# Constant loads placed behind the first input of a Fourier mixer with an MLP

## The chip, the cores and the metric

The kernel runs on one core of a Trainium2 chip. A core has TensorE (PE, matmuls into PSUM), VectorE (DVE) and ScalarE (ACT), which move results from PSUM to SBUF and do elementwise work, GpSimd (POOL) and SyncE (SP). POOL and SP issue most DMAs; 16 DMA engines carry all of them. The metric is the time of one execution on the device in microseconds (us). Before the change it is 810.49 us, the median of three runs from 810.40 to 810.59.

## The reference

Two layers in a row, on 8 sequences of 3008 positions with 256 channels, all float32:

```python
X = np.fft.rfft(x, axis=1)
Yr = Xr @ w_r - Xi @ w_i + b_r
Yi = Xr @ w_i + Xi @ w_r + b_i
Y  = soft_threshold(Yr, 0.01) + 1j * soft_threshold(Yi, 0.01)
y  = np.fft.irfft(Y, n=3008, axis=1)
...
h = y.reshape(24064, 256) @ w_in          # 256 -> 2048
out = (s * relu(h) ** 2 + b) @ w_out      # 2048 -> 256
```

## The kernel before, in words

**The transform as matmuls.** 3008 is 94 x 32, and each transform goes in two steps. The first is a matrix of 94 rows and 96 columns, `A_t` (23 pairs of frequencies and two real ones, as 24 pairs), applied to x viewed as 94 rows of 32 x 256 values. The second, of length 32 with the twiddle factors in it, has a matrix of its own for each of the 24 pairs q: `F_t` for the real and `F_2` for the imaginary part of the input, and `T_t` for the way back. `C_t` is the last step of the inverse. Everything goes through TensorE in float16 with float32 sums.

**Batch 0 goes alone.** The other batches are spread in small units between the MLP's matmuls of the batch before; their order is written out by hand, and a planner's table says which engine takes which piece of work. Batch 0 has nothing to hide behind, and `first_batch` treats it differently: it mixes the channels between the two forward steps. Its stages are

1. first step: for each group of four n2 (a group is half a tile `x16`, which holds eight), four matmuls for each half of the channels put 384 columns into one bank, and the bank is copied to `ut` by ScalarE or VectorE (`evac`, lines 237 and 239, which picks the engine with less planned work). After each group follow five filler matmuls on a tile of ones (`keep_awake`);
2. for each half of the output channels and each of six groups of four pairs: `mix` (eight matmuls of `ut` with the mixing weights `W_t`; the results leave as `g` on VectorE, with the bias `b_g`, line 620, and on ScalarE, line 617), `fwd_dft` (two matmuls for each pair with `F_t` and `F_2`, and one matmul with the selector `sel_t`, a part of the tile `small`, that adds the bias row `b_h`), the soft threshold (ScalarE line 647, VectorE line 649), and `inv_dft` with `T_t`;
3. the turn with an identity (`eye_t`) and the last step with `C_t`, with the first units of batch 1 between them. The first matmul of the MLP, with `w_in`, follows.

**The loads of batch 0.** POOL issues x in eight pieces of four n2 each (line 367), because these loads turn float32 into float16; then two bias rows (line 406). SP issues, in this order, `A_t` (line 385), the mixing weights `w_r` and `w_i` into `w_st` (line 391), four bias rows (line 399), the first part of `F_c` (line 422) and `sel_t` (line 428). `F_c` is the compact form of the forward matrices of pairs 0 to 11: `place_w` (line 480) turns the weights into float16 on ScalarE, and `place_f` (lines 487 to 491) puts the blocks of `F_c` into `F_t` and `F_2`, which were cleared before. A copy of one half goes through ScalarE, the other through VectorE, and the part for `F_2` is four operations on VectorE.

**What holds loads back.** The kernel delays a load by a tiny write: a memset of one element of the destination is queued on VectorE behind a certain eviction, and the DMA must wait for that memset. After the second tile of x, the second part of `F_c` (pairs 4 to 11) is let go in this way (line 586), and the weights are placed; after the third tile the tables `T_t`, `F_t` for pairs 12 to 23, `F_2[1]` and the rest (lines 431 to 441, memsets at line 580), and the first part of `F_c` is placed. The second part of `F_c` is placed after the evictions of the first `mix`. POOL waits with x of batch 1 and the weights of the MLP for the arrival of that `F_t` (a copy of one element, line 591).

**What sets the order.** Up to the end of `first_batch` the framework orders each engine's instructions: in the order of the text, unless an instruction isn't ready by the framework's own estimate and a later one is. `tc.issue_after` adds an order by hand. Behind `first_batch` the order is the written one.

Of the kernel before, what the change touches and what calls it, by code (L numbers as in the profile page):

```python
# [15 lines left out]
P = 128  # L16
N1 = 94
N2 = 32
# [131 lines left out]
def kernel(  # L150
# [13 lines left out]
    nc = tc.nc  # L164
    B, S, D = x.shape
# [5 lines left out]
    H = NPAIR // 2  # L171
# [4 lines left out]
    A_d = nc.inline_tensor(first.astype(np.float16), name="dft_first").ap()  # L176
# [46 lines left out]
    def matmul(out, lhs, rhs, **how):  # L223
        pump()
        return nc.tensor.matmul(out, lhs, rhs, **how)  # L225
# [7 lines left out]
    def evac(dst, src, cols):  # L233
        ta, td = over["act"] + cols / 1200.0, over["dve"] + cols / 960.0
        if act_first(ta, td):
            work("act", ta)
            return None, nc.scalar.copy(out=dst, in_=src)
        work("dve", td)
        return nc.vector.tensor_copy(out=dst, in_=src), None
# [66 lines left out]
    def mix_bank():  # L306
        return track("psm", 4, pools["m"].tile([P, 512], F32, name="psm", tag="psm"))
# [13 lines left out]
    def one_bank():  # L321
        return track("psf", 2, fpool.tile([P, 512], F32, name="psf", tag="psf"))
# [8 lines left out]
    XCH = 8  # L331
# [25 lines left out]
    def emit_load_x(b, chunks=range(N2 // XCH)):  # L357
        xv = x[b].rearrange("(n1 n2) d -> n1 (n2 d)", n2=N2)
        for c in chunks:
            if b < 2 and c == N2 // XCH - 1:  # L360
                t = x2pool.tile([P, XCH * D], F16, name="x2", tag="x2")
            else:
                t = xpool.tile([P, XCH * D], F16, name="x16", tag="x16")
            parts = 2 if b == 0 else 1
            w = XCH * D // parts
            for i in range(parts):
                nc.gpsimd.dma_start(
                    out=t[0:N1, i * w : (i + 1) * w],
                    in_=xv[:, c * XCH * D + i * w : c * XCH * D + (i + 1) * w],
                )  # L370
            x16[(b, c)] = t

# [3 lines left out]
    def keep_awake(n):  # L376

        ps = other_bank()
        for _ in range(n):
            mm = matmul(ps[:, 0:P], ones, ones, start=True, stop=True)  # L380
        return mm


    A_t = cpool.tile([P, 96], F16, name="A_t")
    nc.sync.dma_start(out=A_t[0:N1, :], in_=A_d)
    emit_load_x(0)
    W_t = cpool.tile([P, DC, 2, D], F16, name="W_t")
    w_st = []
    for w in (w_r, w_i):
        st = rpool.tile([P, DC, D], F32, name="w_st", tag="rt")  # L390
        nc.sync.dma_start(out=st, in_=w.rearrange("(c p) e -> p c e", p=P))
        w_st.append(st)

    b_g = tpool.tile([P, 2, D], F32, name="b_g", tag="tail")
# [5 lines left out]
    F_c = uspool.tile([P, H, 2, N2], F16, name="F_c", tag="us")  # L400
    F_2 = [uspool.tile([P, H, P], F16, name="F_2", tag="us") for _ in range(2)]
# [5 lines left out]
    sel_t = small[:, 1, 0:P]  # L407
# [10 lines left out]
    F_t = cpool.tile([P, NPAIR, P], F16, name="F_t")  # L418
    T_t = cpool.tile([P, NPAIR, P], F16, name="T_t")

    def load_f_c(q):
        nc.sync.dma_start(out=F_c[:, q].rearrange("p q r k -> p q (r k)"), in_=F_d[:, q])

    load_f_c(slice(0, 4))

    def emit_load_forward():
        load_f_c(slice(4, H))
        nc.sync.dma_start(out=sel_t, in_=S_d)

    def emit_load_inverse():  # L430
        nc.sync.dma_start(out=T_t[:, 0:H], in_=t_d[:, 0:H])
        nc.sync.dma_start(out=F_t[:, H:], in_=f_d)
        nc.sync.dma_start(out=F_2[1], in_=f_2_d)
        t_load = nc.sync.dma_start(out=T_t[:, H:], in_=t_d[:, H:])
        with tc.issue_after(t_load.ins):
            nc.sync.dma_start(out=eye_t, in_=E_d)
            nc.sync.dma_start(out=C_t, in_=C_d)
            for i, bv in enumerate((b_r, b_i)):
                nc.sync.dma_start(out=b_st[:, i], in_=bv.unsqueeze(0).to_broadcast([P, D]))
            nc.sync.dma_start(out=s_bc, in_=moe_s.unsqueeze(0).to_broadcast([P, 1]))  # L440
            nc.sync.dma_start(out=bb_bc, in_=moe_b.unsqueeze(0).to_broadcast([P, 1]))
# [36 lines left out]
    def place_w():  # L478
        for i in range(2):
            nc.scalar.copy(out=W_t[:, :, i], in_=w_st[i])  # L480

    def place_f(q):

        for a in range(2):
            r = slice(64 * a, 64 * a + 64)
            copy = nc.scalar.copy if a else nc.vector.tensor_copy
            copy(out=blocks(F_t)[r, q, :, a], in_=F_c[r, q])
            nc.vector.tensor_scalar_mul(
                out=blocks(F_2[0])[r, q, 0, a], in0=F_c[r, q, 1], scalar1=-1.0
            )  # L490
            nc.vector.tensor_copy(out=blocks(F_2[0])[r, q, 1, a], in_=F_c[r, q, 0])
# [58 lines left out]
    def first_batch():  # L550
        ut = ypool.tile([P, DC, 96, N2], F16, name="ut", tag="yt")
        last_dve = last_act = None
        last_pe = keep_awake(40)
        for g in range(N2 // 4):
            c, h = divmod(g, 2)
            for dc in range(DC):
                ps = one_bank() if dc else mix_bank()
                with tc.issue_after(last_pe.ins):
                    for j in range(4):
                        lo = (4 * h + j) * D + dc * P  # L560
                        mm = matmul(
                            ps[:, j * 96 : j * 96 + 96],
                            x16[(0, c)][0:N1, lo : lo + P], A_t[0:N1, :],
                            start=True, stop=True,
                        )
                last_pe = mm
                on_dve, on_act = evac(
                    ut[:, dc, :, 4 * g : 4 * g + 4],
                    ps[:, 0:384].rearrange("p (n k) -> p k n", k=96), 384,
                )  # L570
                last_dve = on_dve or last_dve
                last_act = on_act or last_act
            with tc.issue_after(last_pe.ins):
                last_pe = keep_awake(5)
            if h == 0:
                continue
            if c == 2:
                with tc.issue_after(last_dve.ins):
                    for t in (T_t[:, 0:H], F_t[:, H:], F_2[1], T_t[:, H:]):
                        nc.vector.memset(t[0:1, 0, 0:1], 0.0)  # L580
                emit_load_inverse()
                with tc.issue_after(last_dve.ins), tc.issue_after(last_act.ins):
                    place_f(slice(0, 4))
            if c == 1:
                with tc.issue_after(last_dve.ins):
                    nc.vector.memset(F_c[0:1, 4, 0, 0:1], 0.0)
                emit_load_forward()
                with tc.issue_after(last_act.ins):
                    place_w()

        gate = nc.gpsimd.tensor_copy(out=w_in_t[0][0:1, 0:1], in_=F_t[0:1, H, 0:1])
        with tc.issue_after(gate.ins):
            emit_load_x(1)
            emit_load_weights()
# [128 lines left out]
        for i in range(2 * U + 2):  # L723
# [9 lines left out]
            k = i - U - 2  # L733
# [750 lines left out]
    with tc.tile_pool(name="psm", bufs=4, space=bass.MemoryType.PSUM) as pool:  # L1484
        pools["m"] = pool
        rest, more = first_batch()
# [27 lines left out]
    for b in range(2, B):  # L1514
        s0, s1, s2 = mark[b - 2], mark[b - 1], mark[b]
        p = s1 - s0
# [4 lines left out]
        p = s2 - s1  # L1521
# [11 lines left out]
    for ti in range(ti_n + 1):  # L1533
# [3 lines left out]
        for mc in range(MC):  # L1537
# [10 lines left out]
            n = max(len(units), 1)  # L1548
# [37 lines left out]
```

## Time and profile before

| | us |
|---|---|
| median of three runs | 810.49 |
| the profiled execution | 810.04 |
| its span, from the first to the last instruction | 808.2 |
| TensorE busy in the span | 799.2 |
| VectorE busy | 758.9 |
| ScalarE busy | 749.4 |
| first matmul on x | 5.39 |
| first mixing matmul | 14.54 |
| first matmul of the MLP | 44.85 |

How to read the profile: a timeline line gives the start, the duration, the engine, the line of the kernel, the operation, output <- inputs with their shapes, and how many instructions were merged into it; in brackets stands how long the engine was idle before it and what released it. PEld is TensorE's weight load, which lies beside the matmuls. SPq and POOLq are the issuing of DMAs. The lines of the DMA view give, for a stretch of time, each queue's packets, the MB that it moved, and the time of its packets as a share of all 16 DMA engines; q0 is POOL's queue, q1 is SP's. Matmuls and evictions go through helpers, so many have one line (225 for all matmuls) and are told apart by their tiles.

### The profile page before, as it was taken

Reading aid. Unit: us, or ns where it says so; the run is one execution under the profiler, and the core shown is the slowest. Engines: PE = TensorE matmul, PEld = TensorE weight load, DVE = VectorE, ACT = ScalarE, POOL = GpSimd, SP = SyncE. Lnnn points to the kernel's source line nnn. Section 1 sums busy time; section 2 is a strip of 40 time slices with the busy share of each in tenths; the row PEclk is TensorE's granted clock in tenths of the full one; section 3 lists DMA queues with packets and bytes.
Section 4 is the critical chain, followed back from the end, with each engine's and each line's share of the span. In section 5 each row is a group of like instructions: output and inputs, shape, how many; then the busy total and the mean of one; then the engine's idle time right before and its main releaser. Section 6 shows DMA issues by size and latency. Waiting matters only on the chain.

```text
span 808.2 us, 22126 instructions
## 1 busy us (share of the span) xinstructions
PE 799.2 (99%) x9006; PEld 613.1 (76%) x9006; DVE 758.9 (94%) x1342; ACT 749.4 (93%) x932; POOL 107.0 (13%) x151
## 2 busy tenths in 40 slices
PE   8999999999999999999999999999999999999998
PEld 7857767777777977788777886778867788777876
DVE  5899999999999999999999999999999999999895
ACT  5989999999999999999999999999999999998984
POOL 4540001110110101111011210012000100000000
PEclk9999999999999999999999999999999999999999
DMA  8983387555774658665686666666556434732213
GB/s 205 190 194 78 95 237 184 102 136 153 208 151 86 153 139 226 145 124 113 169 200 145 135 145 161 152 154 136 137 164 177 108 80 119 183 67 58 62 41 79
DMA packets 120766, 112.89 MB, mean 140 GB/s; under 512 B 9933, under 2 KB 98129, under 8 KB 120665
## 3 DMA queue, kind: packets, MB, share of 16 engines
q1 hardware_dynamic: 102409, 80.55, 36.0%
q0 software_dynamic: 18256, 30.94, 23.2%
q8 instruction: 70, 1.15, 0.6%
q14 instruction: 31, 0.25, 0.1%
HBM read 53.52 MB, written 46.66 MB: 124 GB/s over the span
## 4 chain that ended last, share of the span: by engine, by line
PE 93%; DMA 0%; ACT 0%; DVE 0%; issue 0%; DVEq 0%; ACTq 0%
PE psh L225 40%; PE psa L225 34%; PE psf L225 19%; DMA out_dram<-ost 0%; DVE ost L1278 0%; ACT rt L1154 0%; ACT u L288 0%; DVEq L1278 0%; ACTq L1154 0%
## 5 line engine op out<-in xcount | busy, mean ns | idle before, releaser
L225 PE MATMUL psh<-yt,w_in 128*128 128x512 f16 (+3 forms) x1792 | 444.5, 343 | 0.2 <-ACT rt L1154 0.2
L225 PEld LDWEIGHTS <-gt 128*128 128x128 f16 x4400 | 306.7, 98 | 141.7 <-DVE gt L1325 2.4
L1154 ACT ACTIVATE rt<-psh 128x1024 f32<-128x1024 f32 x339 | 346.9, 1025 | 23.7 <-PE psh L225 21.5
L1163 ACT ACTIVATE gt<-rt 128x1024 f16<-128x1024 f32 x277 | 289.6, 1059 | 3.1 <-DVE rt L1156 0.7
L225 PE MATMUL psa<-w_out_t,gt 128*128 128x128 f16 (+1 forms) x2208 | 199.6, 224 | 0.0
L225 PEld LDWEIGHTS <-w_in 128*128 128x128 f16 x1824 | 152.0, 98 | 15.8 <-issue 1.4
L225 PE MATMUL psa<-T_s,gt 128*128 128x128 f16 x1824 | 144.3, 219 | 0.0
L1317 POOL DMA_DIRECT2D gt<-gt x63 | 54.8, 870 | 650.0 <-DVE s L1325 194.3
L1165 DVE TENSOR_TENSOR gt<-rt 128x1024 f16<-128x1024 f32 x99 | 120.0, 1216 | 2.4 <-ACT rt L1154 2.1
L1390 DVE SCALAR_TENSOR_TENSOR ost<-psa,s_bc,bias_bc 128x256 f32<-128x256 f32 x152 | 72.6, 478 | 6.7 <-PE psa L225 5.7
L1325 DVE TENSOR_TENSOR gt<-gt 128x1024 f16<-128x1024 f16 x109 | 74.4, 682 | 0.7
L1390 DVE SCALAR_TENSOR_TENSOR ost<-psa,s_bc,ost 128x256 f32<-128x256 f32 x129 | 61.6, 477 | 4.0 <-PE psa L225 3.8
L1325 DVE TENSOR_TENSOR gt<-gt,s 128x1024 f16<-128x1024 f16 x86 | 58.8, 684 | 1.4 <-PE psf L225 0.8
L1325 DVE TENSOR_TENSOR s<-gt 128x1024 f16<-128x1024 f16 x86 | 58.7, 683 | 0.5 <-ACT gt L1163 0.2
L880 DVE TENSOR_TENSOR ring<-psf,s 128x512 f16<-128x512 f32 x84 | 57.5, 685 | 1.7 <-PE psf L225 1.0
L225 PEld LDWEIGHTS <-s 128*128 128x128 f16 x688 | 45.4, 98 | 17.6
L225 PE MATMUL psa<-T_s,s 128*128 128x128 f16 x688 | 52.4, 219 | 0.0
L225 PE MATMUL psf<-W_g,xf 128*128 128x256 f16 x336 | 50.4, 273 | 0.0
L1156 DVE TENSOR_SCALAR rt<-psh 128x1024 f32<-128x1024 f32 x37 | 45.0, 1219 | 3.3 <-PE psh L225 1.6
L225 PEld LDWEIGHTS <-xf 128*128 128x128 f16 x504 | 44.7, 98 | 3.3
L225 PE MATMUL psf<-x,A_t 94*96 94x512 f16 x103 | 39.3, 382 | 0.3 <-DVE u L288 0.2
L225 PE MATMUL psf<-C_t,vs 96*128 96x96 f16 x484 | 38.3, 205 | 0.3 <-DVE u L288 0.3
(116 smaller groups left out, 836.6 us busy)
## 6 DMA issues: line engine op xcount, KB each, us to landing
out_dram<-ost SPq DMA_DIRECT2D x74, 256.0 KB
gt<-gt POOLq DMA_DIRECT2D x63, 256.0 KB, 4.0
ud<-u SPq DMA_DIRECT2D x56, 192.0 KB
us<-ud SPq DMA_DIRECT2D x28, 384.0 KB
vd<-v SPq DMA_DIRECT2D x42, 256.0 KB
vs<-vd SPq DMA_DIRECT2D x28, 384.0 KB
x<-in_x_dram POOLq DMA_DIRECT2D x56, 188.0 KB, 5.6
ring<-ring SPq DMA_DIRECT2D x120, 64.0 KB
```

The lines of the kernel that those rows point to most:

```text
L225: return nc.tensor.matmul(out, lhs, rhs, **how)
L880: lambda e: nc.vector.tensor_tensor(out=ring[0][:, i % 4], in0=ps, in1=hold[i // 2][:, i % 2].unsqueeze(1).to_broadcast([P, 2, D]), op=ALU ...
L1154: nc.scalar.activation(out=rt, in_=ps, func=AF.Relu)
L1156: nc.vector.tensor_scalar(out=rt, in0=ps, scalar1=0.0, scalar2=None, op0=ALU.max)
L1163: nc.scalar.activation(out=gt, in_=rr, func=AF.Square)
L1165: nc.vector.tensor_tensor(out=gt, in0=rr, in1=rr, op=ALU.mult)
L1317: nc.gpsimd.dma_start(out=a12, in_=a11, accum_op=ALU.add)
L1325: nc.vector.tensor_tensor(out=out, in0=a, in1=b, op=op)
L1390: ins = nc.vector.scalar_tensor_tensor(out=out(), in0=hold[of], scalar=s_bc[0:size], in1=other(), op0=ALU.mult, op1=ALU.add,)
```

## The change

1. `A_t` is issued by SP between `w_r` and `w_i` instead of first.
2. The first part of `F_c` (pairs 0 to 3) is no longer issued at the start; it goes where the second part was, behind the memset after the second tile of x. The second part and `sel_t` go behind the third tile, ahead of the large tables, with memsets of their own.
3. The last piece of x (four n2) is loaded in two pieces of two, and the last group of the first step becomes two groups of two n2, each with its own evictions (192 columns) and its five fillers. The other loads of x keep their sizes.

```diff
-            parts = 2 if b == 0 else 1
-            w = XCH * D // parts
-            for i in range(parts):
+            ends = [0, XCH] if b else [0, 4, 6, 8] if c == N2 // XCH - 1 else [0, 4, 8]
+            for lo, hi in zip(ends, ends[1:]):
+                at = c * XCH * D
                 nc.gpsimd.dma_start(
-                    out=t[0:N1, i * w : (i + 1) * w],
-                    in_=xv[:, c * XCH * D + i * w : c * XCH * D + (i + 1) * w],
+                    out=t[0:N1, lo * D : hi * D], in_=xv[:, at + lo * D : at + hi * D]
                 )
...
     A_t = cpool.tile([P, 96], F16, name="A_t")
-    nc.sync.dma_start(out=A_t[0:N1, :], in_=A_d)
     emit_load_x(0)
...
         nc.sync.dma_start(out=st, in_=w.rearrange("(c p) e -> p c e", p=P))
+        if not w_st:
+            nc.sync.dma_start(out=A_t[0:N1, :], in_=A_d)
         w_st.append(st)
...
-    load_f_c(slice(0, 4))
-
     def emit_load_forward():
+        load_f_c(slice(0, 4))
+
+    def emit_load_inverse():
         load_f_c(slice(4, H))
         nc.sync.dma_start(out=sel_t, in_=S_d)
-
-    def emit_load_inverse():
         nc.sync.dma_start(out=T_t[:, 0:H], in_=t_d[:, 0:H])
...
-        for g in range(N2 // 4):
-            c, h = divmod(g, 2)
+        groups = [(lo, 4) for lo in range(0, N2 - 4, 4)] + [(N2 - 4, 2), (N2 - 2, 2)]
+        for n, k in groups:
+            c, at = divmod(n, XCH)
...
                 on_dve, on_act = evac(
-                    ut[:, dc, :, 4 * g : 4 * g + 4],
-                    ps[:, 0:384].rearrange("p (n k) -> p k n", k=96), 384,
+                    ut[:, dc, :, n : n + k],
+                    ps[:, 0 : 96 * k].rearrange("p (n k) -> p k n", k=96), 96 * k,
                 )
...
-            if h == 0:
+            if at == 0:
                 continue
             if c == 2:
                 with tc.issue_after(last_dve.ins):
-                    for t in (T_t[:, 0:H], F_t[:, H:], F_2[1], T_t[:, H:]):
-                        nc.vector.memset(t[0:1, 0, 0:1], 0.0)
+                    for t in (F_c[:, 4], sel_t, T_t[:, 0:H], F_t[:, H:], F_2[1], T_t[:, H:]):
+                        nc.vector.memset(t[0:1, 0:1, 0:1] if len(t.shape) > 2 else t[0:1, 0:1], 0.0)
                 emit_load_inverse()
...
             if c == 1:
                 with tc.issue_after(last_dve.ins):
-                    nc.vector.memset(F_c[0:1, 4, 0, 0:1], 0.0)
+                    nc.vector.memset(F_c[0:1, 0, 0, 0:1], 0.0)
                 emit_load_forward()
```

More of the change, by code (lines that the diff above doesn't have):

```diff
@@ L558, in first_batch @@
                 with tc.issue_after(last_pe.ins):
-                    for j in range(4):
-                        lo = (4 * h + j) * D + dc * P
+                    for j in range(k):
+                        lo = (at + j) * D + dc * P
                         mm = matmul(
```

## The prediction, made before the change was run

> **What bounds the kernel now.** I read the page's engine table first, then the end of the chain of waits, then the timeline of the first 20 us, where every line of the change lies, and last the DMA traffic of that stretch in short windows.
>
> ```profile
> span 808.2 us, 22126 instructions
> PE 799.2 (99%) x9006; PEld 613.1 (76%) x9006; DVE 758.9 (94%) x1342; ACT 749.4 (93%) x932; POOL 107.0 (13%) x151
> ...
> PE 93%; DMA 0%; ACT 0%; DVE 0%; issue 0%; DVEq 0%; ACTq 0%
> ...
> 44.59 0.04 issue
> ```
>
> TensorE is busy for 99% of the span, and the chain that ends last starts only at 44.59 us. The busy times by stretch say the same: from 44.6 to 800.0 TensorE is busy for 755.09 of 755.40 us. The change touches none of that; it can only move the moment at which that run begins. From 14.5 to 34.0 TensorE is busy for 19.27 of 19.50 us, and from 34.0 to 44.6 VectorE for 10.60 of 10.60. So what moves the first mixing matmul (14.54 us) moves the end by as much. Before it, the core waits for x of batch 0:
>
> ```profile
> 9.68 0.34 PE L225 MATMUL psm<-A_t,x 94*128 94x96 f16 x4 [0.28 <-DMA x<-in_x_dram]
> ...
> 13.62 0.34 PE L225 MATMUL psm<-A_t,x 94*128 94x96 f16 x4 [0.17 <-DMA x<-in_x_dram]
> ...
> 14.00 0.48 ACT L237 CAST ut<-psm 128x384 f16<-128x384 f32 x1 [0.49 <-PE psm L225]
> 14.54 1.92 PE L225 MATMUL psm<-W_t,ut 128*128 128x256 f16 x16
> ```
>
> The fourth piece of x is used at 9.68, the eighth at 13.62, each after a wait for its DMA. The last two evictions end at 14.48 (ScalarE) and 14.73 (VectorE), and the mix starts on the first. In the DMA windows 7.00 to 10.25 and 12.00 to 13.25 the columns are packets, MB, share of 16 engines:
>
> ```profile
> q0 software_dynamic: 336, 0.57, 94.9%
> q1 hardware_dynamic: 287, 0.10, 17.7%
> ```
>
> ```profile
> q0 software_dynamic: 122, 0.10, 48.6%
> q1 hardware_dynamic: 125, 0.11, 26.1%
> ```
>
> Queue q0 is x; q1 is SyncE's. The 0.10 MB of the first window are the first forward block (64 KB) and the selector (32 KB), issued at 3.45 and 3.85, and they move while x fills the engines. The 0.11 MB of the second are the second forward block (128 KB), issued at 10.84, at the tail of x.
>
> **The change part by part.**
>
> *Forward block 0 to 3 and selector out of x's way.* They took 17.7% of 3.25 us, 0.57 us of all 16 engines, 0.42 us of it before 9.25. What runs at x's tail instead, the 64 KB block, has 128 packets like the 128 KB one; the same 64 KB took about 0.3 us of all engines in the first window and the larger took 0.33 (26.1% of 1.25), so nothing is won or lost there. The fourth piece lands 0.42 us earlier, the eighth 0.57. That goes by engine share. If bytes bound x instead, the 96 KB go at the pace of its pieces (each read as 376 KB of float32 and landed as 188 KB of float16, 0.98 us apart: 13.62 less 9.68 over four) and give 0.25 us.
> The Trainium skill ("DMA: Bandwidth & Descriptors", section Specifications) puts the limit of HBM per core at about 358 GB/s, which would make bytes the bound and the saving 98,304 B / 358 GB/s = 0.27 us, so that the sum below would be 0.3 us higher. The rows here show 4 x 385 KB in 3.94 us, 391 GB/s, above that figure, so the measurement decides and the share is taken.
>
> *Mix weights first, A_t second.* A_t moved at 1.50 to 2.25 on an eighth of the engines, two of 16:
>
> ```profile
> q1 hardware_dynamic: 96, 0.02, 11.8%
> ```
>
> On the other 14 the mix weights can begin 0.75 us earlier (1.50 instead of 2.25), which takes up to 0.46 us of their traffic out of the time after 3.25 when x runs. On the two engines that carry A_t the total before x's end is unchanged, and a piece lands with its last engine: I take 0, with 0 and -0.46 as ends. Queued behind A_t on SP are w_i and four bias rows, all of them needed after 10.4. A_t itself: issued at about 1.3, behind 1.0 us of weight data, 0.75 us of its own, landed near 3.7. Its first reader runs at 5.39; that 1.7 us covers it. If the weights did not start early it would land near 5.0 to 5.7, and the first unit would be at most 0.3 late, made up in TensorE's waits of 0.17 to 0.46 us ahead of each later piece.
>
> *A ninth load on POOL.* One more issue of 0.53 us (4.26 over eight) moves the two small bias rows and a 0.97 us memset back. The rows at 5.90 and 7.22 already wait; one piece later is 1.4 us more, about 8.6, still ahead of their reader at 16.52, and the memset ends near 10 against its reader at 16.32. Cost 0.
>
> *Two units of half size at the end.* The last eviction shrinks from 0.48 to about 0.32 us on ScalarE and from 0.56 to 0.36 on VectorE (192 columns fewer at 1200 and 960 columns per us, the kernel's own rates), and four matmuls replace eight. Against it stand five filler matmuls more (0.31 us of weight loads) between the units. I take -0.2, with 0 and -0.4 as ends. The kernel's cost rule gives ScalarE three of the four small evictions and VectorE one; over the first batch VectorE then gets one more eviction of 0.68 us, between 18 and 34 us, where it idles for 2.98 us of the 19.5. Cost 0.
>
> *The wait that is added.* The placing of blocks 0 to 3 read data that lay there since about 9 us:
>
> ```profile
> 12.55 0.40 ACT L487 COPY F_t<-F_c 64x256 f16<-64x256 f16 x1
> 13.03 0.48 ACT L237 CAST ut<-psm 128x384 f16<-128x384 f32 x1
> ```
>
> Now the block is issued where the second one was, at 10.84 less 0.42 = 10.42. That one's packets began 1.4 us after its issue and took about 0.9; with 0.4 for the completion (x's last packets fall in 13.0 to 13.25, its reader starts at 13.62) the block is there at 13.1. The nearest faster row is T_t, issued at 12.83 with packets from 13.75: 0.9 + 0.6 + 0.4 gives 12.3. A slow end, with the 1.5 us that the same 64 KB took in the first window, gives 13.7. I take 13.1, the same place under the same traffic. Queued behind this copy on ScalarE are one full and three small evictions: 13.1 + 0.40 + 0.48 + 3 x 0.32 = 14.94 instead of 14.48 for its last. On VectorE five placing operations (12.77 to 13.52, 0.75 us), then 0.56 and 0.36: 14.77 instead of 14.73. The mix needs VectorE's small eviction first and ScalarE's for the second half of its depth, so it runs 0.2 to 0.3 us later than now. I take +0.25; the ends of 12.3 and 13.7 give -0.5 (set by x again) and +0.85.
>
> *Second block and selector behind it.* Both now go ahead of the four large tables on SP: 0.32 + 0.43 us more issue. The second block would land near 14.5 and the selector near 15; they are read at 16.12 and 16.52. The tables were issued from 12.83, now from about 13.1, at most 0.75 later. POOL's gate waits for F_t, 17.30 before, so x of batch 1 and the MLP weights start up to 0.75 us later. The weights are first read at 44.7 and landed by 36.7 at the latest (issued at 19.85 and 20.42, 16.3 us to land); the inverse table's first reader is at 19.16. Cost 0. If that cover were gone, the 0.75 would count.
>
> **Sum.** x 0.57 earlier and the smaller last unit 0.2 would give -0.77, but the placing stands in between and sets +0.25. The profiled execution took 810.04 (808.2 plus 1.84 around it), so 810.29; it lies 0.45 below the median of 810.49, which gives 810.7.
>
> **The rivals.** *The placing lets the evictions pass.* TensorE's order shows that the planner moves work past what isn't ready: half a mix stands ahead of the first inverse product, and the selector's load stands far ahead of its place in the text. If the placing comes after the last evictions, it fits the idle 1.36 us of ScalarE and 0.78 of VectorE at 14.5 to 15.8, and x decides: -0.77, 809.7, between -0.3 and -1.4. Against it: before the change the placing came in the order of the text, and two pieces of x (2 us) lie between issue and use.
>
> *The block comes late.* Slower than before. The first load of this block began to move 3.5 us after its issue and took 1.5. From 10.42 that is 15.9 with completion, and the mix starts 3.2 us later: 813.7. It is slower than before from a landing at 12.85, and by over 0.2% (1.6 us, about what a measurement of this kernel can tell from no change) from 14.3, that is 3.9 us after issue. Against it: then w_i and four rows stood ahead in the queue, now nothing does.
>
> *All gains in full.* 0.57 + 0.46 from the early weights + 0.4 from the unit, with evictions passing, and 0.33 if the block at x's tail now falls behind it: -1.76, 808.7. It needs the two engines of A_t not to hold a piece back.
>
> **How the numbers follow.** Forecast 0.50 (its own range 810.0 to 811.3), evictions passing 0.33, late block 0.10, all gains 0.07. The first two lie within 0.2%, so same is 0.83, faster 0.07, slower 0.10. The range of 809.2 to 811.6 leaves out the last two rivals and the rim of the second.
>
> **What would show it.** The fourth piece's matmul near 9.3 and the last near 13.1; SyncE's q1 nearly empty from 7 to 10; an idle of 0.5 to 1 us ahead of the copy at L487 put down to the DMA of the forward block; the first mixing matmul near 14.8; the chain's start moved by as much. A mix before 14.0 speaks for the passing evictions, one after 16 for the late block. A gap anywhere after 45 us that is new would make the whole reading wrong.

## The result, and the profile after

The changed kernel takes 811.79 us (median of 22 executions, 810.99 to 812.75) against 810.42 us for the kernel before (22 executions): a ratio of 1.0016, 95% interval 1.0010 to 1.0022. It is 1.37 us slower; the prediction was 810.7 us, and 811.79 lies just above its range. Single executions of one kernel spread over 1 to 3 us, so below a time goes with its median and interval, and a reading with the rows of one profiled execution. That of the changed kernel took 811.42 us, 1.38 more than the one of before.

The page of the changed kernel shows as much TensorE work as before (799.2) in a span that is 1.4 us longer:

```profile
span 809.6 us, 22144 instructions
...
PE 798.8 (99%) x9011; PEld 614.0 (76%) x9011; DVE 759.5 (94%) x1345; ACT 749.6 (93%) x933; POOL 107.5 (13%) x152
```

The chain that ends last (start, duration, what) now passes through a load that was on no chain before, the first forward block:

```profile
1.92 5.38 DMA x<-in_x_dram
...
10.93 3.42 DMA F_c<-dft_fwd
15.72 1.91 PE psm L225 x16
```

And the timeline shows both halves of the change, the last unit of x earlier (13.14; 13.62 before) and the first mixing matmul later (15.72; 14.54 before), with the wait between them:

```profile
9.44 0.53 PE L225 MATMUL psm<-A_t,x 94*128 94x96 f16 x4
...
13.14 0.25 PE L225 MATMUL psm<-A_t,x 94*128 94x96 f16 x2
...
14.44 0.40 ACT L486 COPY F_t<-F_c 64x256 f16<-64x256 f16 x1 [0.91 <-DMA F_c<-dft_fwd]
...
14.45 0.22 DVE L486 COPY F_t<-F_c 64x256 f16<-64x256 f16 x1 [1.28 <-DMA F_c<-dft_fwd]
...
15.21 0.36 DVE L239 CAST ut<-psm 128x192 f16<-128x192 f32 x1
...
15.72 1.47 PE L225 MATMUL psm<-W_t,ut 128*128 128x256 f16 x12 [1.96 <-DVE ut L239]
```

x is all there by 13.14, where its last unit starts without a wait. Both copy engines stand idle until the block lands at 14.4, place it, and only then make the last small evictions that the mix waits for. The DMA windows 7.00 to 10.25 and 12.00 to 13.25 of the changed kernel (packets, MB, share of 16 engines) say that the loads did get out of x's way: q1 is empty in the first, and the block moves at x's tail in the second.

```profile
q0 software_dynamic: 380, 0.64, 113.0%
q1 hardware_dynamic: 1, 0.00, 0.0%
```

```profile
q0 software_dynamic: 122, 0.05, 30.5%
q1 hardware_dynamic: 136, 0.06, 17.2%
```

How the landing at 14.4 comes about stands in two more windows of the changed kernel, 12.00 to 12.85 and 12.85 to 13.57:

```profile
q0 software_dynamic: 122, 0.05, 44.9%
q1 hardware_dynamic: 135, 0.06, 24.7%
q8 instruction: 1, 0.02, 6.8%
```

```profile
q1 hardware_dynamic: 7, 0.00, 4.3%
```

By the packet sizes in the trace the block is 128 packets of 512 B on q1. Of these, 120 start from 12.08 to 12.82. The last eight, a sixteenth of the block, start one after the other from 13.19 to 13.59; the last ends at 13.66, and the copies start at 14.44, 0.78 later. Just ahead of the eight ends the one packet of q8, a load of 16 KB that the profile calls "instruction": 6.8% of 16 engines over 0.85 us is 0.92 us of one engine, and in the trace it lasts from 12.28 to 13.21. So it seems that this packet holds one of the 16 DMA engines, and that engine's share of the block stands behind it. The trace doesn't name the engines, so this is argued from the times.

Of the delay, 1.18 us is there at the first mix. VectorE's first multiplication of the MLP (line 1165) starts at 49.17 instead of 47.73, +1.44; the outputs are 1.43 later at 68.5 us and 1.37 later at the end. So nothing new happens in the long run of matmuls: from 45.72 to 800.00 TensorE is busy for 753.49 of 754.28 us.

### The profile page after: what moved, and what is told of

Same layout as the page of the kernel before. It is cut to its first block, busy times and chain, and to the rows that moved or that the text cites. A ratio compares the mean times of both kernels' runs of the same rounds, so it can differ in the third digit from the quotient of the medians.

```text
span 809.6 us, 22144 instructions
## 1 busy us (share of the span) xinstructions
PE 798.8 (99%) x9011; PEld 614.0 (76%) x9011; DVE 759.5 (94%) x1345; ACT 749.6 (93%) x933; POOL 107.5 (13%) x152
## 3 DMA queue, kind: packets, MB, share of 16 engines
q8 instruction: 70, 1.15, 0.6%
## 4 chain that ended last, share of the span: by engine, by line
PE 96%; DMA 1%; DVE 1%; ACT 0%; issue 0%; POOL 0%; DVEq 0%; ACTq 0%; POOLq 0%
PE psh L225 40%; PE psa L225 34%; PE psf L225 20%; PE psm L225 1%; DMA x<-in_x_dram 1%; DMA F_c<-dft_fwd 0%; DMA out_dram<-ost 0%; DVE u L288 0%; ACT m L647 0%; DVE yt L288 0%; DVE z L649 0%; DVE vs L288 0%; DVE vt L239 0%; DVE ost L1278 0%; ACT rt L1154 0%
```

## The experiments

All times are medians; "before" is the kernel before, run on the same chip beside them. The last three columns are rows of the one profiled execution: the last unit of x, the first mixing matmul, and how much later than in the kernel before the outputs come at 68.5 us. Up to 400 us this shift stays as it is. At the end of the span it is within 0.15 us of the column, but for e7 (+1.75), e8 (+2.03), g1 (+0.70) and h1 (+0.85); what adds to it there, no run shows.

| kernel | us | before | ratio, 95% interval | last x | mix | shift |
|---|---|---|---|---|---|---|
| changed | 811.79 | 810.42 | 1.0016, 1.0010 to 1.0022 | 13.14 | 15.72 | +1.43 |
| e1 block at the start | 811.15 | 810.22 | 1.0008, 0.9999 to 1.0016 | 15.26 | 16.05 | +2.43 |
| e2 placing late | 810.58 | 810.22 | 1.0004, 0.9995 to 1.0013 | 13.59 | 14.38 | +0.44 |
| e3 load moves only | 811.16 | 810.22 | 1.0008, 0.9999 to 1.0016 | 13.50 | 14.40 | +1.82 |
| e4 halved unit only | 810.78 | 810.22 | 1.0002, 0.9994 to 1.0011 | 13.42 | 14.38 | +0.56 |
| e5 swap only | 810.81 | 810.16 | 1.0005, 0.9996 to 1.0014 | 14.55 | 15.47 | +1.02 |
| e6 A_t first | 811.58 | 810.70 | 1.0011, 1.0002 to 1.0020 | 13.26 | 15.67 | +1.40 |
| e7 more fillers | 812.73 | 810.16 | 1.0028, 1.0017 to 1.0039 | 14.28 | 15.48 | +1.20 |
| e8 released early | 812.98 | 810.16 | 1.0030, 1.0021 to 1.0039 | 13.32 | 15.66 | +1.57 |
| e10 POOL later | 811.56 | 810.16 | 1.0015, 1.0007 to 1.0024 | 14.81 | 15.98 | +2.83 |
| f1 moves, placing late | 811.38 | 810.70 | 1.0008, 0.9999 to 1.0017 | 13.01 | 13.92 | +1.11 |
| f2 f1 and sum first | 811.43 | 810.70 | 1.0006, 0.9997 to 1.0015 | 12.79 | 13.71 | +1.12 |
| f3 sum first only | 811.77 | 810.70 | 1.0017, 1.0008 to 1.0026 | 14.54 | 15.71 | +3.18 |
| g1 f1, tables unmoved | 810.31 | 810.42 | 1.0000, 0.9991 to 1.0009 | 13.23 | 14.14 | +0.52 |
| h1 changed, all mended | 810.86 | 810.42 | 1.0004, 0.9996 to 1.0013 | 13.85 | 14.64 | +0.50 |
| i1 g1, block by POOL | 810.31 | 810.29 | 1.0002, 0.9993 to 1.0011 | 13.11 | 14.02 | -0.29 |
| i2 changed, block by POOL | 812.04 | 810.29 | 1.0025, 1.0016 to 1.0034 | 14.08 | 15.78 | +1.61 |

Most intervals are 1.4 us wide, as much as the whole effect. They tell the changed kernel, e6, e7, e8, e10, f3 and i2 from the kernel before; the verdicts on the others rest on rows. In these rows the granted clock of TensorE has a part too: before 16.5 us it was at half for 6.8 us in the profiled executions of e1, e10 and f3, for 3.4 us in those of the changed kernel, e2, e3, e5 and g1, and not at all between 7 and 800 us in the others.

### The parts alone: e3, e4, e5

e3 is the kernel before with the moves of the two blocks and the selector, e4 with the two half units and the two half loads, e5 with `A_t` behind `w_r`; each is that part of the change's diff and nothing else.

> The kernel before, with the moves of the forward blocks and the selector alone. Theory: the block lands 3.4 us after its issue, at 13.9 to 14.3, five placing operations and one whole eviction follow on VectorE, so that the mix's second half waits to 15.3 or later: 0.5 to 1.0 us slower than before (1.0006 to 1.0012). Rival (the other two parts cost the time): the same as before or faster.

> The kernel before, with the split of the last piece of x and its units alone. Theory: the last unit ends 0.1 to 0.3 us earlier, and the new order up to the MLP gives 0.2 us back: within 0.2 us of before (0.9998 to 1.0002). Rival (the ninth load or the order that follows from the split costs the time): 0.5 us or more slower (1.0006 or more).

> The kernel before, with A_t behind w_r alone. First reading (A_t's two engines hold the first piece of x back, and the gap lets TensorE's clock fall): first matmul on x at 5.6 us or later instead of 5.3 to 5.5, the second near 7.4, and a granted clock of 0.50 over about 3.4 us somewhere between 7 and 14; the mix up to 0.5 us later or unchanged, the time 0 to 0.6 us longer (1.0000 to 1.0007). Second reading (the weights' earlier start relieves x): mix at 14.3 or earlier and the time 0.2 us shorter.

The moves alone reproduce the wait (ScalarE's copy at 14.67, VectorE's at 14.69 after 0.71 us idle). Here the first half of the mix starts at 14.40, but one VectorE eviction stands behind the placing and the rest of the mix waits for it; the first forward product comes at 17.39, 1.10 later than before.

```profile
16.07 1.48 PE L225 MATMUL psm<-W_t,ut 128*128 128x256 f16 x12 [1.06 <-DVE ut L239]
```

The halved unit does on the first mixing matmul what was forecast, -0.16 (14.38), but the first forward product comes at 16.32, 0.03 later than before. And on VectorE, in e4:

```profile
46.12 0.69 DVE L288 CAST u<-psa 96x512 f16<-96x512 f32 x1 [0.18 <-PE psa L225]
...
48.03 1.63 DVE L1165 TENSOR_TENSOR gt<-rt 128x1024 f16<-128x1024 f32 x1
```

The first multiplication starts at 48.03 instead of 47.73: it seems that the smaller evictions change which engine takes which later piece: VectorE, which was busy for all of 34.0 to 44.6 before, is now idle for 0.27 of it and behind by 0.30. So -0.16 turns into +0.30. The median is 0.56 above the kernel before, inside its interval. The 1.63 us, instead of 1.21, are taken up below.

The swap alone gains nothing at x's end. Its first unit waits for x, not for `A_t`:

```profile
6.26 0.34 PE L225 MATMUL psm<-A_t,x 94*128 94x96 f16 x4 [0.99 <-DMA x<-in_x_dram]
```

In the seven profiled executions with the swap the first unit starts at 5.66 to 6.70, in the eleven without at 5.28 to 5.89. What the swap costs at the mix isn't separated: e5's clock was at half in part of this stretch, of which more below.

### The wait: e1, e2, e6, e8, e7

e1 is the changed kernel with the first block loaded at the start again:

```diff
-    def emit_load_forward():
-        load_f_c(slice(0, 4))
+    load_f_c(slice(0, 4))
...
-                with tc.issue_after(last_dve.ins):
-                    nc.vector.memset(F_c[0:1, 0, 0, 0:1], 0.0)
-                emit_load_forward()
```

> The changed kernel, but forward block 0 to 3 loaded at the start again. Theory (the late block holds the placing, the placing holds the last evictions): no wait ahead of the copies into F_t, first mixing matmul at 14.0 to 14.3, MLP run starting about where it did before, so 0.1 to 0.4 us faster than the kernel before (ratio 0.9995 to 0.9999). Rival (the other parts cost the time: half units, ninth load, selector and second block ahead of the tables, A_t behind the weights): still 0.8 us or more slower than before (1.001 or more).

The wait for the block is gone (the copy runs at 13.75 behind nothing). But this profiled execution lost 2 us elsewhere: from 8 to 14 us its TensorE clock was granted at 0.50, and the units, 1.17 us apart, became the bound. The median, 0.93 above before against 1.37, agrees with a wait that costs something and settles no size.

e2 is the changed kernel with the placing told to follow the last evictions:

```diff
-                with tc.issue_after(last_dve.ins), tc.issue_after(last_act.ins):
-                    place_f(slice(0, 4))
...
+        with tc.issue_after(last_dve.ins), tc.issue_after(last_act.ins):
+            place_f(slice(0, 4))
```

> The changed kernel with the same loads, but the placing of blocks 0 to 3 put behind the last evictions on both engines. Theory: the block still lands at about 14.4, nobody is queued behind it; first mixing matmul at 13.9, the first forward product still after 15.2 and so not held; 0.2 to 0.6 us faster than before (0.9993 to 0.9998). Rival (the late block delays the mix through something other than the order on the two engines, or the other parts cost the time): no better than 0.5 us slower than before.

```profile
13.64 0.65 ACT L237 CAST ut<-psf 128x192 f16<-128x192 f32 x2
14.56 0.40 ACT L486 COPY F_t<-F_c 64x256 f16<-64x256 f16 x1 [0.27 <-DMA F_c<-dft_fwd]
```

The block is as late as before this edit (14.56), and all small evictions now precede it. The mix starts at 14.38 and about 1 us of the 1.37 is back, in the median (+0.36) as in the shift (+0.44). This is the run that shows the cause: not the block's lateness by itself but what stands behind it. It shows it by its rows; the intervals of e2 and of the changed kernel overlap.

e6 puts `A_t` first again and leaves the rest of the change:

> The changed kernel with the forward matrix A_t loaded first again, as before the change. Theory that A_t behind the mix weights delays the first piece of x and with it opens the idle time after which the granted clock falls: first unit at 5.3 to 5.5 instead of 5.7, the clock at 1.00 more often, block issued at 10.4 to 10.9, the block still lands near 14; time 0 to 0.4 below the changed kernel, still 0.7 to 1.4 above the kernel before. Theory that the swap alone is to blame for the loss: back at the kernel before's time, within 0.3.

```profile
13.26 0.25 PE L225 MATMUL psm<-A_t,x 94*128 94x96 f16 x2
...
14.39 0.40 ACT L485 COPY F_t<-F_c 64x256 f16<-64x256 f16 x1 [0.75 <-DMA F_c<-dft_fwd]
...
15.67 1.58 PE L225 MATMUL psm<-W_t,ut 128*128 128x256 f16 x13 [1.80 <-DVE ut L239]
```

This is the cleanest picture. The clock is 1.00 throughout, the block is issued at 10.49, as forecast, and it is still there only at 14.39. The mix and the shift (+1.40) are those of the changed kernel, so neither the swap nor the clock is needed for the loss.

e8 lets the block go behind the first tile of x instead of the second:

> The changed kernel with the first block let go behind the first tile of x (about 8.6 us) instead of the second. If the time from issue to landing is about 3.4 us wherever it stands: there by 12.0 to 12.6, no wait or under 0.3 us ahead of the placing, mix at 13.8 to 14.3 (later where the clock falls), 0.2 to 0.6 us slower than before through the order alone (1.0002 to 1.0008). If the block only lands once x is through: there at 14 to 14.5, mix after 15.3, 1.2 us or more slower (1.0015).

```profile
8.40 4.34 SPq L422 DMA_DIRECT2D F_c<-dft_fwd  x2
```

```profile
q1 hardware_dynamic: 10, 0.00, 1.0%
```

```profile
13.89 0.40 ACT L486 COPY F_t<-F_c 64x256 f16<-64x256 f16 x1 [1.80 <-DMA F_c<-dft_fwd]
```

Issued more than two us earlier, at 8.40, it lands at 13.89. The second line is q1 from 8.40 to 11.75: ten packets in 3.35 us, while POOL's q0 fills the engines (108.8%). In every kernel here whose copy waits for this load on SyncE, with issues from 8.40 to 11.31, it lands at 13.9 to 15.0, never before x is through: the issue doesn't set it. In seven of these eight executions (all but e8) the block's last eight packets begin within 0.03 us of the end of the instruction packet, which ends at 12.8 (f2) to 13.8 us (g1). In e8 the block's last packet has ended at 13.03, ahead of that. In all eight the copies start 0.70 to 0.86 us after the block's last packet. Being early even hurt at the engines, because the framework then put the placing ahead of six evictions; in the changed kernel two stand behind it. The median, 2.82 above the kernel before, is more than this execution's 2.01, and no run shows why.

e7 gives TensorE 56 fillers at the start and nine behind each of the first five units:

> The changed kernel with 56 filler matmuls at the start instead of 40, and nine instead of five behind each of the first five units. If the clock of 0.50 between 7 and 11 us delays the units and with them the block's issue: clock 1.00 throughout, the block issued at 10.4 to 10.6 instead of 10.93, mix 0.3 to 0.5 us earlier than in the changed kernel, and 0.3 to 0.6 us off its median excess of 1.4 over the kernel before (1.0010 to 1.0014 here). If the clock is a bystander: mix and time as in the changed kernel.

The clock stays at 1.00 and the block is issued at 10.56, but the seventh piece of x is late (13.20, after 1.14 us of waiting), the placing (14.11) stands ahead of all four small evictions, and the mix comes at 15.48. The median, 2.57 above the kernel before, is the second worst. More fillers are no cure, and the clock isn't what holds the mix here.

### Why an earlier mix brings nothing: e10, f1, f2, f3, g1, h1

e2 and e4 left a loss of 0.4 to 0.6 us although their mix was earlier than before. In both, multiplications at line 1165 are stretched beside POOL's sum of the rows of `w_out` (line 520 or 521). e10 asks for that directly: before, with two dummy additions ahead of the sum.

> The kernel before with two more additions of 1.16 us on POOL ahead of its sum of w_out (their result is overwritten), so that the sum ends near 50.2 instead of 47.8 and lies beside VectorE's first multiplications from SBUF (line 1165 before, from 47.73). If POOL and VectorE slow each other there, as 1.63 instead of 1.21 us in the kernel with the split alone suggests: those multiplications take 0.3 to 0.8 us longer together, and the end moves by 0.3 to 0.8 us (1.0004 to 1.0010), with the mix and the MLP's start where they were. If not: the same time as before.

The kernel before has

```profile
46.68 1.16 POOL L521 TENSOR_TENSOR small<-acc,w_out_t 128x512 f16<-128x512 f32 x1
47.73 1.21 DVE L1165 TENSOR_TENSOR gt<-rt 128x1024 f16<-128x1024 f32 x1
49.58 2.35 DVE L1165 TENSOR_TENSOR gt<-rt 128x1024 f16<-128x1024 f32 x2
```

and e10 has

```profile
51.24 3.57 DVE L1169 TENSOR_TENSOR gt<-rt 128x1024 f16<-128x1024 f32 x2
51.71 2.02 POOL L525 TENSOR_TENSOR small<-acc,w_out_t 128x512 f16<-128x512 f32 x1
```

VectorE's pair of multiplications takes 3.57 us instead of 2.35, and three of POOL's additions 4.79 instead of 3.5. That is more than the 0.3 to 0.8 us expected, and it agrees with the median (+1.40). Of the shift of 2.83, 1.44 is there at the mix already, in a stretch where this execution's clock was at half. f1 is the kernel before with the load moves and the placing behind the evictions (e3 with e2's edit):

> The kernel before with the load moves alone (no halved unit, no swap), and the placing of blocks 0 to 3 told to follow the last two evictions on both engines. Theory that the wait for the late block is the cost and the earlier x is a real gain: x about 0.5 us earlier, block still there only near 14.4, the placing then in the engines' idle time behind the evictions; first mixing matmul at 13.9 to 14.2, and the time 0.3 to 0.6 below the kernel before. Theory that an earlier mix is given back to VectorE's multiplications that then run beside POOL's sum of w_out: mix as early, but at 68 us no more than 0.2 is left, time within -0.3 and +0.2 of before. Theory that x gains nothing from the moves: mix at 14.4 to 14.6, time +0 to +0.3.

```profile
18.83 0.18 POOL L590 COPY w_in<-F_t 1x1 f16<-1x1 f16 x1 [9.80 <-DMA F_t<-fwd_rest]
...
46.21 3.69 POOL L520 TENSOR_TENSOR acc<-acc,w_out_t 128x512 f32<-128x512 f32 x2
...
49.51 3.57 DVE L1164 TENSOR_TENSOR gt<-rt 128x1024 f16<-128x1024 f32 x2
...
49.98 2.02 POOL L520 TENSOR_TENSOR small<-acc,w_out_t 128x512 f16<-128x512 f32 x1
```

The mix is 0.62 earlier; the MLP only 0.07, since the placing, at 14.80, now holds the first forward product; and then the pair loses 1.22 us. The reason lies thirty us back, where the kernel before has

```profile
17.30 0.18 POOL L591 COPY w_in<-F_t 1x1 f16<-1x1 f16 x1 [8.61 <-DMA F_t<-fwd_rest]
```

In f1 the second block and the selector stand ahead of the tables on SyncE, `F_t` lands 1.5 us later, POOL's gate opens at 18.83 instead of 17.30, the weights' loads follow it, and the sum ends at 52.0 instead of 47.84, on top of the multiplications.

f2 lets the sum go ahead of POOL's loads of x of batch 2; f3 does that alone, in the kernel before:

```diff
+                with tc.issue_after(sum_last[0].ins):
                     nc.gpsimd.dma_start(out=t[0:N1, i * w : (i + 1) * w], in_=xv[:, at : at + w])
```

> As the run above, and POOL's sum of the rows of w_out stands ahead of its loads of x of batch 2, so that it should end some 1.7 us earlier, near 46. Theory that POOL's sum stretches VectorE's multiplications when the MLP starts early: these multiplications take 1.2 us again, and the time is 0.3 to 0.6 below the run above and 0.3 to 0.9 below the kernel before. Theory that the stretch has nothing to do with POOL: same as the run above.

> The kernel before with only the sum of w_out moved ahead of the loads of x of batch 2 on POOL. There the sum ends at 47.84 and the first multiplications begin near 47.7, so hardly anything overlaps. Theory of the collision: within 0.2 us of before, at most 0.3 below. Rival, that the order on POOL delays x of batch 2 enough to be felt: slower by over 0.3.

```profile
48.75 2.35 DVE L1168 TENSOR_TENSOR gt<-rt 128x1024 f16<-128x1024 f32 x2
...
58.75 0.40 PE L225 MATMUL psf<-F_t,us 128*128 128x128 f16 x4 [1.77 <-DMA us<-ud]
```

Both lines are of f2. The stretch is gone, as the theory of the collision says, and the 0.83 us gained at the mix is still there at 56.8. Then a new wait of 1.8 us takes it: x of batch 2 is loaded from 46.96 on, the DMA engines are full from 50 to 54 us (a share of 1.06 and 1.00 in the two halves, 0.47 and 0.27 in the kernel before), which seems to hold the writes to `ud`, and SyncE issues the loads of `us` at 55.55 instead of 52.23. f3 shows that this comes without the change too: there `us` is issued at 57.57, and the kernel is slower by 1.07 us. (1.17 of f3's shift of 3.18 is there at the mix, where its clock was at half.) The forecast of "within 0.2" for it was wrong.

g1 mends the gate instead: f1 with the second block and the selector let go together with the first block.

```diff
     def emit_load_forward():
         load_f_c(slice(0, 4))
+        load_f_c(slice(4, H))
+        nc.sync.dma_start(out=sel_t, in_=S_d)
 
     def emit_load_inverse():
-        load_f_c(slice(4, H))
-        nc.sync.dma_start(out=sel_t, in_=S_d)
```

> As the run with the moves alone and the placing behind the last evictions, but the second forward block and the selector are let go together with the first block, so that SyncE issues the tables' first load near 12.8 as before the change, and not at 14.1. Theory that the tables' delay is what turns the earlier start into a loss: POOL's gate near 17.3, the last load of w_out at 28 to 28.5, the sum of w_out done near 47.8, VectorE's pair of multiplications back to 2.35 us (from 3.57), and the time 0.8 to 1.4 below the run with the tables late, so 0 to 0.6 below the kernel before. Theory that the delay has another source (x's own pace, POOL's waits for x of batch 1): gate at 18 or later, multiplications still above 3 us, time as in that run.

```profile
17.46 0.18 POOL L591 COPY w_in<-F_t 1x1 f16<-1x1 f16 x1 [8.28 <-DMA F_t<-fwd_rest]
```

```profile
47.83 1.78 DVE L1165 TENSOR_TENSOR gt<-rt 128x1024 f16<-128x1024 f32 x1
...
50.14 2.34 DVE L1165 TENSOR_TENSOR gt<-rt 128x1024 f16<-128x1024 f32 x2
```

The tables go at 12.84, the gate opens at 17.46, the sum ends at 48.53, the pair is back to 2.34, and the median is the kernel before's. This confirms the chain from tables to multiplications. What is left of the collision is the first multiplication (1.78 instead of 1.21). And the mix, 0.40 earlier than before, is given back sooner: the placing, at 14.97, holds the first forward product until 16.50, 0.21 later than before.

h1 is the changed kernel with all three mends (`A_t` first, g1's release, e2's placing):

> The changed kernel with A_t first, both blocks and the selector let go together, and the placing of the first block behind the last evictions. Theory that the late block and the late tables are together the whole loss: first mixing matmul at 13.8 to 14.2, multiplications unstretched, 0.2 to 0.7 below the kernel before. Rival, that the halved unit's order keeps VectorE later whatever x does: mix as early, but at 68 us within 0.2 of before or 0.2 to 0.6 later.

The multiplications take 1.50 and 2.34 us, and the mix comes at 14.64 instead of the 13.8 to 14.2 expected, because x itself ended late in this execution (13.85). The rival of the halved unit isn't excluded: +0.50 at 68.5 us. The kernel is not better than before.

### Through POOL's queue: i1, i2

Does the block land late because SyncE carries it, or does everything at x's tail? i1 is g1 and i2 the changed kernel, each with the first block issued by POOL behind x and the bias rows:

```diff
-        load_f_c(slice(0, 4))
...
+    nc.gpsimd.dma_start(
+        out=F_c[:, 0:4].rearrange("p q r k -> p q (r k)"), in_=F_d[:, 0:4]
+    )
```

> As the run with the tables unmoved and the placing behind the last evictions, but the first forward block is issued by POOL behind x and its two bias rows. Theory that the lateness belongs to SyncE's load beside POOL's full queue: the block moves directly behind x and is there by 13.9, the placing waits for nothing (about 14.2 instead of 14.97, behind the evictions), the first forward product follows the first mix by 1.75 us as before the change and not by 2.36, and the time is 0.2 to 0.6 below that run. Theory that whatever moves at x's tail lands late: the copy still waits until 14.4 or later.

```profile
13.99 0.40 ACT L489 COPY F_t<-F_c 64x256 f16<-64x256 f16 x1
...
14.02 1.92 PE L225 MATMUL psm<-W_t,ut 128*128 128x256 f16 x16
...
15.78 0.22 PE L225 MATMUL psf<-g,F_t 128*128 128x128 f16 x1
```

> The changed kernel with the first forward block issued by POOL behind x and the bias rows; the placing stands where the change has it. Theory of SyncE's queue: the block lands at 13.0 to 13.9, the first mixing matmul at 14.5 to 15.2 (instead of 15.72), the time 0.5 to 1.2 below the changed kernel. Theory that the tail of x is slow for everything: mix at 15.5 or later, time as the changed kernel.

```profile
14.60 0.22 DVE L486 COPY F_t<-F_c 64x256 f16<-64x256 f16 x1 [0.49 <-DMA F_c<-dft_fwd]
```

In i1 the copy waits for nothing at 13.99, and the forward product follows the mix by 1.76 us again, as before. This is the only profiled execution below the kernel before's (-0.29 at 68.5 us, span 808.0 against 808.2); by the medians the two can't be told apart, and the 0.2 to 0.6 us under g1 didn't show there. i2 went against the forecast of the theory of SyncE's queue and with its rival's (mix at 15.78, median 1.75 above the kernel before). POOL could issue the ninth piece of x only at 6.50 and the block at 10.40, x's last unit ran at 14.08, and the copy on VectorE started at 14.60.

In POOL's queue the block's last packet ends at 12.74 (i1) and 13.87 (i2), and the trace has its landing 0.97 and 0.63 us later, 13.71 and 14.50. On SyncE it is 0.70 to 0.86 from the last packet to the copy. So the completion isn't what the two queues differ in. What differs is when the last packets move: 14.21 is the end of the last one in g1, 12.74 in i1, where none stands behind the instruction packet (12.35 to 13.32). What stays open is why SyncE's block moves only when POOL's queue thins out, and no run moves the instruction packet itself.

## Why the prediction was wrong, point by point

**x 0.42 and 0.57 earlier: right.** q1 was empty from 7 to 10.25. Where nothing else disturbs it, in f2, the fourth unit starts at 9.13 and the eighth at 12.79, 0.55 and 0.83 earlier; in f1 0.52 and 0.61. So the share of the engines was the better measure, and the saving by bytes (0.25) was too small.

**A_t second, 0: if anything the wrong side of its ends.** e5 shows no gain at x's end, and the first unit is later in most executions with the swap. The cover of 1.7 us for `A_t` held; it was the first piece of x that came late.

**Ninth load, 0: held in the changed kernel** (POOL's memset ends at 9.90, needed at 16.3); in i2, with one more load behind, it no longer did.

**Half units, -0.2: right at the first mixing matmul (-0.16), wrong at the first forward product (+0.03) and by 47 us.** "One more eviction between 18 and 34 us, cost 0" left out that the planner's choices shift after it: +0.46 on VectorE. In the changed kernel the like is 0.26, from +1.18 at the mix to +1.44 at the first multiplication.

**The added wait, +0.25: the step that failed.** Its working was issue 10.42, packets 1.4 later, 0.9 long, 0.4 for the completion: 13.1. Measured in the changed kernel: issue 10.93 (10.49 in e6, at full clock), first packet 1.15 later at 12.08, 1.58 to the end of the last packet at 13.66, and 0.78 to the copies at 14.44. So the terms were off by +0.51, -0.25, +0.68 and +0.38, and two of them were wrong in the working itself. The 0.9 was read from the second block in the window 12.00 to 13.25, whose 0.11 MB were taken for the whole block; but 128 KB are 0.131 MB. The rest moves behind that window; this is SyncE's queue in the kernel before from 13.25 to 13.75:

```profile
q1 hardware_dynamic: 12, 0.01, 9.3%
```

The last of the second block's 128 packets starts at 14.24, and eight of them stand one after the other behind the instruction packet, which ends at 13.50. From the first packet, 1.1 us after the issue, to the end of the last are 2.3 us, not 0.9. The 0.4 was taken from x, whose reader starts 0.3 us after the end of its last packet (13.30), and used for a load of SyncE's, where it is 0.70 to 0.86. The slow end of 13.7 had the packets about right (1.5) and kept the 0.4. The late block's chance of 0.10 was too low: the landing came 3.5 us after the issue (3.9 in e6). The place is that rival's; the size lies between it and the forecast.

**Evictions passing: half of it.** Three of ScalarE's four and one of VectorE's two last evictions passed the placing, but one on each did not, and the mix needs both. So a landing at 14.44 cost 1.18 at the mix and not the 1.59 that the working gives (14.44 less 12.85, from which the loss was to begin). By the same working the late block's threshold of 14.3 should read 14.45.

**Second block, selector, tables, 0: right in the changed kernel, for a reason not given.** The gate opened at 17.88 (+0.58, within the 0.75), but the chain named, up to the weights' reader at 44.7, wasn't the tight one. It is POOL's sum, which ends at 47.84 beside multiplications that start at 47.73. In the changed kernel the sum ends 1.35 later (49.19) and VectorE is 1.44 later, and they barely touch. The versions that keep the mix early and leave the sum where it is pay there: +1.22 in f1, and 0.3 to 0.6 in e2, e4, g1 and i1.

**The sum.** x's gain of 0.6 could not be had: behind the placing it is hidden, and past the placing it runs VectorE into POOL. Only i1's profiled execution kept a part of it (0.29), which its median doesn't show.

## What to carry to other kernels

A load lands with its last packet: before a window is taken for a load, add up its MB until they are the load's size, look for a long packet of another queue (here an instruction load of 0.93 us) that can hold a part of it back, and take the completion from a load on the same queue. Then look at what stands behind its first reader on that reader's engine. Where a load must come late, put its reader behind the work that doesn't need it (e2: 1 us of 1.37 back for two lines moved). And before a stage is credited with an earlier start, look which off-path engine ends just ahead of the next stage's work on a port or queue that they share; here a margin of 0.1 us decided.

## What the runs showed of the hardware that was not expected

**One instruction packet seems to hold one DMA engine for 0.9 us.** In each of the 18 profiled executions a packet of 16 KB on q8 moves once between 11 and 14 us, for 0.88 to 0.97 us. In seven of them the last eight of the block's 128 packets begin within 0.03 us of its end, and in the kernel before it is so with eight packets of the second block. So a load of 64 KB, whose other packets need 0.7 us in the changed kernel, lands as late as this one packet lets it. That both stand on the same engine is argued from the times.

**A SyncE load can stand nearly still beside POOL's full queue.** Ten packets of q1 beside 451 of q0 in 3.35 us in e8 (8.40 to 11.75), until x thins out. In the kernel before, a load issued at 3.45 begins to move at 7.02, and from 7.00 to 10.25 there are 287 packets of q1 beside 336 of q0. The Trainium skill ("DMA: Bandwidth & Descriptors", section Queues, rings and completion order) says that each engine takes turns between the queues at packet granularity; the second row agrees, the first doesn't show such turns, and whether the block's packets stood in the engines' queues by then, no trace shows. The same section says that a load's semaphore write lands only after every earlier write of that DMA engine, across its queues. The changed kernel agrees: of the 16 packets of 4 B that q1 moves beside the block's, 15 start by 12.84 and the last at 13.64, behind the eight late ones. Why the completion then takes 0.7 to 0.9 us on SyncE and 0.3 for x stays open.

**VectorE's multiplication and POOL's addition take turns.** Line 1165 multiplies a tile in SBUF by itself. The pair grows from 2.35 to 3.57 us in e10 and f1, by 1.22, about one POOL addition (1.17); POOL's last addition grows from 1.16 to 2.02. The Trainium skill ("SBUF — State Buffer", section Who interferes with whom) has it that a VectorE instruction with two SBUF inputs contends with a POOL instruction that reads SBUF, and that the ports they share are an exclusive lock; these numbers agree.

**The TensorE clock can fall to half behind a stretch with little work.** In windows of the changed kernel's profile:

```profile
7.00:8.00 1.00, 0.66 (x11) 0.66 (x12) 0.03 (x1) 0.28 (x1) 0.16 (x1) 0.82 1.21 205
8.00:11.00 3.00, 3.00 (x36) 3.00 (x34) 1.65 (x4) 1.68 (x5) 1.81 (x3) 0.50 1.09 194
11.00:12.00 1.00, 1.00 (x23) 1.00 (x22) 0.57 (x2) 1.00 (x3) 0.00 (x0) 0.98 1.07 177
```

The column behind POOL's busy time, 0.82, 0.50 and 0.98, is the granted clock: 0.36, 3.00 and 0.04 us at half, 3.4 in all. The units then come 1.17 us apart and bound the stage, which made the block's issue 0.5 us late here. It was at half for 6.8 us in e1, e10 and f3, and not between 7 and 800 us in ten of the 18. In the eight executions with a fall TensorE was busy for 1.2 to 2.0 us of the 3.4 us ahead of it. In the others, over the first 3.4 us that the profile records at full clock, it was busy for 2.1 to 3.4 us, but for e6 and h1 (1.96 and 1.79, no fall). So little work goes with the fall without settling it. Of the changed kernel's 22 executions, the seven with a mean clock of 1.000 have a median of 811.20 us and the eleven with 0.998 one of 811.80, so the clock is a part of the spread. The Trainium skill ("TensorE: Matmul & The Clock Gate", Part 1) gives a window of about 3.4 us that runs free of the kernel; the length agrees.
